# Performer attention and a gated feed-forward block on one Trainium2 core: k chunks taken in opposite order by two engines, loads gated to the projection phase, crossbar transposes moved to the gate phase

## The chip, the cores and the metric

The kernel runs on one core of one Trainium2 chip. The metric is device time in microseconds (us); lower is better. Each time is the median of several executions. The profile of one execution is shown beside it; its span is about 1.8 us shorter than the time of the same execution.

Names: TensorE (PE, with its weight loads PEld) multiplies matrices; VectorE (DVE) and ScalarE (ACT) work elementwise and reduce; POOL is GpSimd, which here issues the loads and builds the identity matrix; SP (SyncE) issues stores and crossbar transposes (a DMA that transposes on its way). PSUM is the memory into which TensorE writes.

Tiles: `pk` and `pq` are the projections of k and q, each taken in five chunks per batch; `k_p` and `q_pT` their exponentials; `v_ext` is v times the weights `wk`; `kz` holds kv and z; `nd` numerator and denominator of the attention, `xt` (`xT`) its transpose; `g_ps` and `v_ps` are the gate and value products, `o_ps` the last projection.

## The reference, cut to what matters

```python
# q, k, v: (8, 8, 576, 64); omega: (128, 64)
def phi(x):
    proj = einsum('bhsd,md->bhsm', x, omega)
    h = proj - sum(x * x, -1) / 2
    return exp(h - max(h, -1)) / sqrt(m)
q_p, k_p = phi(q * scale), phi(k * scale)
kv, z = einsum('bhsm,bhsd->bhmd', k_p, v), sum(k_p, 2)
attn  = einsum('bhsm,bhmd->bhsd', q_p, kv) / (q_p . z + 1e-6)
x   = attn as (4608 tokens, 512)
out = (gelu(x @ w_gate) * (x @ w_val)) @ w_out      # d_ff = 1536
```

## The kernel before

Attention of batch t + 1 is woven into the feed-forward of token tile t (512 tokens). The kernel has a start (attention of batches 0 and 1, gates of tile 0), six steps with attention (t = 1 to 6), two without, and an end (the last projection). Within a step comes first the *projection phase* (48 `o_ps` matmuls of tile t - 1, with k and q chunks between them), then the *gate phase* (12 pairs of `g_ps` and `v_ps`, with `kz` and `nd` between them). The order on PE, ACT and DVE is the program's order.

```python
att = tc.tile_pool(name="att", bufs=2, space=PSUM)   # 2 tiles of 2 banks
mo  = tc.tile_pool(name="mo",  bufs=4, space=PSUM)   # 4 tiles of 1 bank

def k_chunk(self, c):
    i0, n = CHUNKS[c]
    pk = att_tile([P, 2, 4, M], F32, "pk")
    ...                                              # 2n matmuls into pk
    nc.scalar.activation(self.k_p[...], pk[:, :, :n, :], func=Exp)
    nc.vector.reduce_max(self.nmax[...], pk[:, :, :n, :], axis=AX, negate=True)

# end of start(): tile 0's first gates, batch 1's last k chunk done
        n.weights()          # wk = exp(-max), on ACT
        g.gelu(0)
        n.v_half(0)          # v_ext = v * wk, on DVE
        g.mul(0)
        g.gelu(1)
        g.val(1)
        n.v_half(1)
        g.mul(1)
        n.kz()               # needs v_ext
        for jf in range(2, N_DFF): ...

def step(t, before):
    p = Projection(t - 1, before.gated)
    ...
    load_batch(t + 2)                                # k, q, v by POOL
    a = Attention(t + 1)
    a.kT, a.qT = transposed_dma("k", t + 1), transposed_dma("q", t + 1)   # by SP
    a.k_chunk(0); a.k_chunk(1); p.go(15)
    a.k_chunk(2); a.k_chunk(3); p.go(13)
    ...
```

A chunk's `pk` is free for the next chunk but one when both its exponential and its maximum are done.

The softmax here doesn't subtract the row's maximum and nothing guards it: scores larger than these inputs give would overflow.

## Time and profile before

| | before |
|---|---|
| time, median | 368.79 us (3 runs), 368.91 us (4 runs) |
| span of the profile | 366.3 us |
| start, to the first `pk` of step 1 | 63.72 us |
| one step (2 to 6), first `pk` to first `pk` | 37.44 us |
| a step without attention | 31.1 us |
| last matmul to the end of the span | 5.5 us |

Three lines of the page of before: busy time (with the share of the span and the number of instructions), the granted clock of TensorE in 40 equal slices in tenths of full speed (9 is 90% or more), and the engines' shares of the chain of waits that ended last.

```profile
...
PE 344.7 (94%) x2673; PEld 165.6 (45%) x2673; DVE 207.4 (57%) x336; ACT 161.5 (44%) x259; POOL 26.0 (7%) x40
...
PEclk9989699999999999999999999999999999999999
...
PE 78%; DVE 8%; ACT 7%; DMA 5%; issue 1%; POOL 0%; POOLq 0%
...
```

TensorE is busy nearly all the time and carries most of the chain. So a gain has to come from TensorE's waits, or from its clock: one slice, at 37 to 46 us, reads 6.

The timeline of before, TensorE in step 2's projection phase. Columns: start, length, engine, line, operation, output<-inputs, shape, count, and in brackets the idle time ahead and what ended it.

```profile
...
100.99 0.62 PE L196 MATMUL pk<-omegaT_106,kT 64*128 64x128 bf16 x16
101.55 3.41 PE L337 MATMUL o_ps<-w_out_sb,gated 128*128 128x512 bf16 x15
104.89 0.40 PE L196 MATMUL pk<-omegaT_106,kT 64*128 64x128 bf16 x8
105.61 0.40 PE L196 MATMUL pk<-omegaT_106,kT 64*128 64x128 bf16 x8 [0.32 <-DVE nmax L198]
105.94 2.98 PE L337 MATMUL o_ps<-w_out_sb,gated 128*128 128x512 bf16 x13
...
```

The first 16 `pk` matmuls fill both tiles and take 0.56 us (101.55 - 100.99). The next 16 take 1.05 us (105.94 - 104.89): the last eight wait for VectorE's maximum (`nmax`) of an earlier chunk. The waits of the whole kernel (total us, times, longest) say why the maximum comes late:

```profile
...
DVE nmax L198 <- ACT k_p L197: 15.9, 22, 1.8
...
```

It waits for the exponential of the same chunk. Both engines only read, but they read the same PSUM banks. The Trainium skill, "PSUM — Partial Sum Buffer", section "PSUM bank collisions raise a hardware error", says that two engines must not read one bank at once, so the program puts one behind the other; this trace agrees with the 15.9 us above.

The chain of waits of before in the start (start, length, what):

```profile
...
40.41 1.17 PE kz_ps L236 x36
41.58 1.82 PE g_ps L291 x4
43.40 1.62 PE v_ps L304 x4
...
48.48 15.19 DMA kT<-k_in
...
63.72 0.28 PE pk L196 x4
```

`kz` of batch 1 runs at half speed (1.17 us for 36), and so do the next eight gate matmuls (1.82 and 1.62 us for four each; warm it is 0.86). Then, at the end of the start, stands a crossbar transpose that took 15.19 us from issue to landing; TensorE had other work for nearly all of that time and waited only 0.47 us for it. The windows view of before shows the clock (the number ahead of the last two):

```profile
...
core 0: us, PE busy (x) PEld busy (x) DVE busy (x) ACT busy (x) POOL busy (x), PEclk, DMA share, GB/s
36.00:38.00 2.00, 0.09 (x6) 0.10 (x8) 1.55 (x3) 1.89 (x3) 0.64 (x1) 1.00 1.24 207
...
40.00:42.00 2.00, 1.59 (x38) 1.22 (x38) 1.27 (x4) 0.00 (x0) 0.00 (x0) 0.50 1.26 216
...
44.00:46.00 2.00, 2.00 (x16) 0.96 (x15) 0.84 (x3) 0.03 (x1) 0.00 (x0) 0.80 1.23 209
...
```

TensorE idled before (0.09 us busy in 36 to 38), and the clock fell to 0.50 for some 6.8 us. The chain at the end of before:

```profile
...
350.44 10.37 PE o_ps L337 x48
...
360.83 0.69 DVE o_sb L341
```

### The profile page before, as it was taken

How to read it: one execution, taken by the hardware profiler on the slowest of the kernel's cores; microseconds unless marked ns; L12 is line 12 of the kernel's file. 1: busy time of each engine (PE TensorE's matmuls, PEld its weight loads, DVE VectorE, ACT ScalarE, POOL GpSimd, SP SyncE). 2: the span in 40 equal slices, each digit the busy share in tenths (PEclk: the TensorE clock that was granted, in tenths of full speed). 3: DMA queues.
4: the chain of work that ended last, by engine and by line, in shares of the span. 5: the costliest groups of instructions: out<-in, count | busy, mean ns of one | idle time of the engine just before them, and what ended most of it. 6: DMA issues, size and time to landing. Idle time of an engine off the chain costs nothing.

```text
span 366.3 us, 6525 instructions
## 1 busy us (share of the span) xinstructions
PE 344.7 (94%) x2673; PEld 165.6 (45%) x2673; DVE 207.4 (57%) x336; ACT 161.5 (44%) x259; POOL 26.0 (7%) x40
## 2 busy tenths in 40 slices
PE   3787799999999999999999999999999999999993
PEld 2463454445444544354435443544354444444441
DVE  2977584758475847574666567655856333424431
ACT  4877224662367336643664365536453113303310
POOL 8223000201001000100000000000000000000000
PEclk9989699999999999999999999999999999999999
DMA  7999999999618981799079206420312040031013
GB/s 119 271 272 207 207 271 185 249 283 235 87 30 215 209 117 29 185 221 135 23 159 216 44 6 154 104 50 0 87 38 58 7 109 1 1 74 42 0 30 87
DMA packets 64238, 44.11 MB, mean 120 GB/s; under 512 B 44752, under 2 KB 57552, under 8 KB 64208
## 3 DMA queue, kind: packets, MB, share of 16 engines
q0 software_dynamic: 15392, 23.60, 32.0%
q1 hardware_dynamic: 48816, 20.10, 27.6%
q8 instruction: 21, 0.34, 0.4%
q14 instruction: 9, 0.07, 0.1%
HBM read 37.78 MB, written 9.44 MB: 129 GB/s over the span
## 4 chain that ended last, share of the span: by engine, by line
PE 78%; DVE 8%; ACT 7%; DMA 5%; issue 1%; POOL 0%; POOLq 0%
PE g_ps L291 24%; PE v_ps L304 23%; PE o_ps L337 21%; DVE nmax L198 6%; DMA kT<-k_in 4%; PE kz_ps L236 3%; ACT k_p L197 3%; PE nd L251 2%; PE pq L210 2%; PE pk L196 2%; ACT L197 2%; DVE x_sb L259 1%; DMA k_in<-in_k_dram 1%; ACT g_gelu L297 1%; ACT q_pT L213 1%
## 5 line engine op out<-in xcount | busy, mean ns | idle before, releaser
L309 DVE TENSOR_TENSOR gated<-g_gelu,v_ps 128x512 bf16<-128x512 bf16 x108 | 73.7, 687 | 102.1 <-PE v_ps L304 77.3
L297 ACT ACTIVATE g_gelu<-g_ps 128x512 bf16<-128x512 f32 x108 | 63.7, 597 | 142.0 <-PE g_ps L291 141.9
L291 PE MATMUL g_ps<-xT,w_gate_sb 128*128 128x512 bf16 x432 | 111.9, 382 | 0.0
L304 PE MATMUL v_ps<-xT,w_val_sb 128*128 128x512 bf16 x432 | 111.7, 381 | 0.0
L337 PE MATMUL o_ps<-w_out_sb,gated 128*128 128x512 bf16 x432 | 97.9, 380 | 0.0
L304 PEld LDWEIGHTS <-w_val_sb 128*128 128x128 bf16 x432 | 41.8, 98 | 51.9 <-issue 3.0
L337 PEld LDWEIGHTS <-gated 128*128 128x128 bf16 x432 | 40.3, 98 | 50.7 <-issue 4.1
L291 PEld LDWEIGHTS <-w_gate_sb 128*128 128x128 bf16 x432 | 39.6, 98 | 43.1 <-issue 0.6
L198 DVE TENSOR_REDUCE nmax<-pk 128x8 f32<-128x1024 f32 (+1 forms) x40 | 43.3, 1114 | 16.0 <-ACT k_p L197 15.9
L213 ACT ACTIVATE q_pT<-pq 128x512 bf16<-128x512 f32 (+1 forms) x80 | 38.2, 564 | 16.6 <-PE pq L210 16.6
L197 ACT ACTIVATE k_p<-pk 128x1024 bf16<-128x1024 f32 (+1 forms) x40 | 36.1, 937 | 21.0 <-PE pk L196 20.7
L341 DVE COPY o_sb<-o_ps 128x512 f32<-128x512 f32 x36 | 24.7, 686 | 23.5 <-PE o_ps L337 23.0
L259 DVE TENSOR_TENSOR x_sb<-nd,iden 128x512 bf16<-128x512 f32 (+3 forms) x45 | 28.4, 631 | 1.5
L224 DVE TENSOR_TENSOR v_ext<-vf,wk 128x1152 bf16<-128x1152 f32 x16 | 21.7, 1358 | 2.8 <-ACT wk L202 2.8
L196 PE MATMUL pk<-omegaT_106,kT 64*128 64x128 bf16 x288 | 14.9, 228 | 3.8 <-DVE nmax L198 3.0
L251 PEld LDWEIGHTS <-q_pT 128*128 128x128 bf16 (+1 forms) x320 | 13.8, 100 | 10.2 <-DVE x_sb L259 2.5
L251 PE MATMUL nd<-kz,q_pT 128*128 128x65 bf16 (+1 forms) x320 | 15.9, 194 | 0.6 <-ACT kT L163 0.6
L236 PE MATMUL kz_ps<-v_ext,k_p 64*128 64x65 bf16 x576 | 12.5, 203 | 3.9 <-DVE v_ext L226 3.9
L196 PEld LDWEIGHTS <-kT 64*128 64x128 bf16 x288 | 9.3, 97 | 14.6 <-issue 12.6
L236 PEld LDWEIGHTS <-k_p 64*128 64x128 bf16 x576 | 11.4, 103 | 7.1 <-issue 4.0
L210 PE MATMUL pq<-qT,omegaT_106 64*128 64x512 bf16 (+1 forms) x80 | 12.7, 363 | 1.8 <-ACT q_pT L213 1.4
L93 POOL DMA_DIRECT2D vf<-in_v_dram x8 | 6.1, 765 | 78.8 <-DVE v_ext L226 77.0
(34 smaller groups left out, 95.8 us busy)
## 6 DMA issues: line engine op xcount, KB each, us to landing
vf<-in_v_dram POOLq DMA_DIRECT2D x8, 1152.0 KB, 7.7
out_dram<-o_sb SPq DMA_DIRECT2D x72, 128.0 KB, 2.4
q_in<-in_q_dram POOLq DMA_DIRECT2D x8, 576.0 KB, 10.0
k_in<-in_k_dram POOLq DMA_DIRECT2D x7, 576.0 KB, 11.1
w_gate_sb<-in_moe_w_gate_dram POOLq DMA_DIRECT2D x3, 512.0 KB, 20.9
w_val_sb<-in_moe_w_val_dram POOLq DMA_DIRECT2D x3, 512.0 KB, 20.7
w_out_sb<-in_moe_w_out_dram POOLq DMA_DIRECT2D x3, 512.0 KB, 20.3
k_in<-in_k_dram POOLq DMA_DIRECT2D x2, 288.0 KB, 4.7
```

The costliest lines, as they stand in the source:

```text
L196: nc.tensor.matmul(pk[:, a, i, :], self.kT[sl, i0 + i, :], omegaT2[sl])
L197: nc.scalar.activation(self.k_p[:, :, i0:i0 + n, :], pk[:, :, :n, :], func=Exp)
L198: nc.vector.reduce_max(self.nmax[:, :, i0:i0 + n], pk[:, :, :n, :], axis=AX, negate=True)
L213: nc.scalar.activation(dst[:, a, i0:i0 + n], pq[:, a, :n, :].rearrange("m i (e p) -> m i e p", e=2), func=Exp)
L236: nc.tensor.matmul(kz_ps[e][:, j * DP1:(j + 1) * DP1], self.k_p[sl, u % 2, u // 2, :], self.ve[sl, u, :], start=(r == 0), stop=(r == R - 1))
L251: nc.tensor.matmul(nd[h // 4][:n, (h % 4) * DP1:(h % 4 + 1) * DP1], self.q_pT[:, e, u:u + nr, :].rearrange("m r p -> m (r p)"), self.kz_sb ...
L259: nc.vector.tensor_mul(x_sb[:n].rearrange("p (g h d) -> p g h d", g=2, h=4)[:, gs], ndv[:, :, :, :D], iden[:n, gs].broadcast_to((n, gs.sto ...
L291: nc.tensor.matmul(g_ps, w_gate_sb[:, jm, fs], self.xT[:, jm, :], start=(jm == 0), stop=(jm == N_DM - 1))
L297: nc.scalar.activation(g_gelu, self.ps[jf], func=Gelu)
L304: nc.tensor.matmul(v_ps, w_val_sb[:, jm, fs], self.xT[:, jm, :], start=(jm == 0), stop=(jm == N_DM - 1))
L309: nc.vector.tensor_mul(self.gated[:, jf, :], self.gelus[jf], self.vps[jf])
L337: nc.tensor.matmul(self.o_ps, self.gated[:, jf, qq * P:(qq + 1) * P], w_out_sb[:, jf, :], start=(jf == 0), stop=(jf == N_DFF - 1))
```

## The change

Its intent: (1) the two engines take a pair of chunks in opposite order, so that neither waits for the other at the beginning; (2) the loads of batch t + 2 wait for the first exponential of step t, and the crossbar transposes come in the gate phase before they are needed; (3) in the start: the first k load ahead of the identity, `kz` of batch 0 in two halves, two qT copies moved from VectorE or later, `kz` of batch 1 behind two more gate pairs, batch 2 loaded ahead of the output weights; (4) at the end, the last 128 tokens in two half-width pieces whose stores go out on two queues.

```diff
+        def k_pair(self, c):
+            p0, p1 = self.k_proj(c), self.k_proj(c + 1)
+            begun = self.k_exp(*p0)
+            self.k_max(*p1)
+            self.k_exp(*p1)
+            self.k_max(*p0)
+            return begun
 ... loads of the start
-    ident = singles.tile([P, P], BF16); make_identity(nc, ident)
     load_kq("k", 0, parts=2)
+    ident = singles.tile([P, P], BF16); make_identity(nc, ident)
     load_kq("q", 0)
 ...
     load_gv(2)
+    load_kq("k", 2)
+    load_kq("q", 2)
     ...                                  # w_out
+    load_v(2)
 ... start()
         a.q_chunk(2)
+        a.kz(0)
         ...
         qp(1, dve)
+        a.kz(1)
         a.q_chunk(4)
-        a.kz()
-        qp(2, act)
-        qp(3, dve)
         n.q_chunk(0)
         a.nd(0)
         n.q_chunk(1)
+        qp(2, act)
         a.nd(1)
         a.xt(0)
+        qp(3, act)
 ...
-        n.v_half(0)
         g.mul(0)
+        n.v_half(0)
         ...
-        n.kz()
         for jf in range(2, N_DFF):
             g.both(jf)
-            if jf < 7: n.nd(jf - 2)
-            if 2 < jf < 8: n.xt(jf - 3)
+            if jf == 3: n.kz()
+            if 4 <= jf < 9: n.nd(jf - 4)
+            if 5 <= jf < 10: n.xt(jf - 5)
+            if jf == 5: kqT["k", 2] = transposed_dma("k", 2)
+            if jf == 9: kqT["q", 2] = transposed_dma("q", 2)
 ... step()
-        load_batch(t + 2)
-        a.kT, a.qT = transposed_dma("k", t + 1), transposed_dma("q", t + 1)
-        a.k_chunk(0)
-        a.k_chunk(1)
+        a.kT, a.qT = kqT.pop(("k", t + 1)), kqT.pop(("q", t + 1))
+        begun = a.k_pair(0)
+        load_batch(t + 2, begun)         # each load depends on begun
         p.go(15)
-        a.k_chunk(2)
-        a.k_chunk(3)
+        a.k_pair(2)
 ... after a.kz(): kqT["k", t + 2] = transposed_dma("k", t + 2); q's after jf == 5
-    with tc.manual_schedule(engines={E.Activation, E.PE, E.DVE}):
+    with tc.manual_schedule(engines={E.Activation, E.PE, E.DVE, E.SP}):
 ...
-        Projection(N_TOK - 1, g.gated).go(NSUB * N_DFF)
+        Projection(N_TOK - 1, g.gated).end()   # last piece 2 x 256 columns, stores on SP and ACT
```

More of the change, by code (lines that the diff above doesn't have):

```diff
@@ L70, in mo_tile @@
         return mo.tile(shape, dtype, name=name, tag="mo")
-    ident = singles.tile([P, P], BF16)
-    make_identity(nc, ident)
     def rows_of(src, b):
@@ L85, in load_kq @@
         n = HP // parts
-        for c in range(parts):
-            nc.gpsimd.dma_start(out=tv[:, c * n:(c + 1) * n],
-                                in_=rows_of(src, b)[:, c * n:(c + 1) * n])
         loaded[nm, b] = t
+        return [nc.gpsimd.dma_start(out=tv[:, c * n:(c + 1) * n],
+                                    in_=rows_of(src, b)[:, c * n:(c + 1) * n])
+                for c in range(parts)]
     def load_v(b):
         t = ld.tile([P, HP, R * D], F32, name="vf")
-        nc.gpsimd.dma_start(out=t, in_=rows_of(v, b))
         loaded["v", b] = t
+        return [nc.gpsimd.dma_start(out=t, in_=rows_of(v, b))]
     w_gate_sb = singles.tile([P, N_DM, d_ff], BF16)
@@ L110 @@
     load_kq("k", 0, parts=2)
+    ident = singles.tile([P, P], BF16)
+    make_identity(nc, ident)
     load_kq("q", 0)
@@ L187, in two_banks, with k_proj @@
             return [t[:, 0], t[:, 1]], [(slice(0, 2), t)]
-        def k_chunk(self, c):
+        def k_proj(self, c):
             i0, n = CHUNKS[c]
@@ L196, in k_chunk, with k_exp, k_max @@
                     nc.tensor.matmul(pk[:, a, i, :], self.kT[sl, i0 + i, :], omegaT2[sl])
-            nc.scalar.activation(self.k_p[:, :, i0:i0 + n, :], pk[:, :, :n, :], func=Exp)
+            return c, pk
+        def k_exp(self, c, pk):
+            i0, n = CHUNKS[c]
+            return nc.scalar.activation(self.k_p[:, :, i0:i0 + n, :], pk[:, :, :n, :],
+                                        func=Exp)
+        def k_max(self, c, pk):
+            i0, n = CHUNKS[c]
             nc.vector.reduce_max(self.nmax[:, :, i0:i0 + n], pk[:, :, :n, :], axis=AX,
                                  negate=True)
+        def k_chunk(self, c):
+            p = self.k_proj(c)
+            self.k_exp(*p)
+            self.k_max(*p)
+        def k_pair(self, c):
[5 more added lines that the diff above has]
+            return begun
         def weights(self):
@@ L226, in v_half, with kz @@
             nc.vector.tensor_copy(vev[:, isl, :, D], wkv[:, isl])
-        def kz(self):
-            kz_ps, groups = self.two_banks("kz_ps")
-            for j in range(HP):
+        def kz(self, half=None):
+            if half != 1:
+                self.kz_ps = self.two_banks("kz_ps")
+            kz_ps, groups = self.kz_ps
+            for j in range(HP) if half is None else range(2 * half, 2 * half + 2):
                 for r in range(R):
@@ L238, in kz @@
                                          start=(r == 0), stop=(r == R - 1))
-            for gs, t in groups:
+            for gs, t in groups if half != 0 else ():
                 nc.vector.tensor_copy(self.kz_sb[:, gs], t[:, :, :HP * DP1])
@@ L315, in both, with store @@
             self.mul(jf)
-    def store(c0, o_sb):
+    def store(c0, o_sb, ns=slice(0, d_model), queues=(nc.sync, nc.sync)):
         g = c0 // SP
@@ L321, in store @@
             b, r = divmod(g + i, R)
-            nc.sync.dma_start(
-                out=out[b * S:(b + 1) * S, :].rearrange("(p r) m -> r p m", r=R)[r],
+            queues[i].dma_start(
+                out=out[b * S:(b + 1) * S, ns].rearrange("(p r) m -> r p m", r=R)[r],
                 in_=o_sb[i * SP:(i + 1) * SP, :])
@@ L330, in __init__, with end @@
             self.t, self.gated, self.done = t, gated, 0
+        def end(self):
+            self.go((NSUB - 1) * N_DFF)
+            n = d_model // 2
+            for half in range(2):
+                ns = slice(half * n, (half + 1) * n)
+                o_ps = mo_tile([P, n], F32, "o_ps")
+                for jf in range(N_DFF):
+                    nc.tensor.matmul(o_ps, self.gated[:, jf, (NSUB - 1) * P:NSUB * P],
+                                     w_out_sb[:, jf, ns], start=(jf == 0),
+                                     stop=(jf == N_DFF - 1))
+                o_sb = work.tile([P, n], F32, name="o_sb", bufs=3)
+                nc.vector.tensor_copy(o_sb, o_ps)
+                store(self.t * T_TOK + (NSUB - 1) * P, o_sb, ns, (nc.sync, nc.scalar))
         def go(self, n):
@@ L343, in go, with load_batch @@
                 self.done += 1
-    def load_batch(b):
-        load_kq("k", b)
-        load_kq("q", b)
-        load_v(b)
+    kqT = {}
+    def load_batch(b, begun):
+        for dma in load_kq("k", b) + load_kq("q", b) + load_v(b):
+            tc.add_manual_dep(dma.ins, begun.ins.name, mybir.DependencyInfo(
+                mybir.DependencyClass.Sync, mybir.DependencyReason.DATA))
     def start():
@@ L406, in start @@
         n.k_chunk(1)
-        load_batch(2)
         g = Gated(0)
@@ L416, in start @@
         g.gelu(0)
+        g.mul(0)
         n.v_half(0)
-        g.mul(0)
         g.gelu(1)
         g.val(1)
+        g.mul(1)
         n.v_half(1)
-        g.mul(1)
-        n.kz()
         for jf in range(2, N_DFF):
             g.both(jf)
-            if jf < 7:
-                n.nd(jf - 2)
-            if 2 < jf < 8:
-                n.xt(jf - 3)
+            if jf == 3:
+                n.kz()
+            if 4 <= jf < 9:
+                n.nd(jf - 4)
+            if 5 <= jf < 10:
+                n.xt(jf - 5)
+            if jf == 5:
+                kqT["k", 2] = transposed_dma("k", 2)
+            if jf == 9:
+                kqT["q", 2] = transposed_dma("q", 2)
         return g
@@ L441, in step @@
             return g
+        a = Attention(t + 1)
+        a.kT, a.qT = kqT.pop(("k", t + 1)), kqT.pop(("q", t + 1))
+        begun = a.k_pair(0)
         if t + 2 < B:
-            load_batch(t + 2)
-        a = Attention(t + 1)
-        a.kT, a.qT = transposed_dma("k", t + 1), transposed_dma("q", t + 1)
-        a.k_chunk(0)
-        a.k_chunk(1)
+            load_batch(t + 2, begun)
         p.go(15)
-        a.k_chunk(2)
-        a.k_chunk(3)
+        a.k_pair(2)
         p.go(13)
@@ L469, in step @@
         a.kz()
+        if t + 2 < B:
+            kqT["k", t + 2] = transposed_dma("k", t + 2)
         for jf in range(2, N_DFF):
@@ L475, in step @@
                 a.nd(jf - 1)
+            if jf == 5 and t + 2 < B:
+                kqT["q", t + 2] = transposed_dma("q", t + 2)
         return g
     E = mybir.EngineType
-    with tc.manual_schedule(engines={E.Activation, E.PE, E.DVE}):
+    with tc.manual_schedule(engines={E.Activation, E.PE, E.DVE, E.SP}):
         g = start()
```

## The prediction

> **What bounds the kernel now.** TensorE: the page gives it 344.7 of 366.3 us busy and 78% of the chain of waits. The chain has four stretches: a start up to 63.1 us, six steps of 37.45 us (first `pk` matmul at 100.99, 138.44, ...), two steps of 31.1 us without attention, and an end from 350.3 us. Only TensorE's remaining waits can be won:
>
> 1. Steps 2 to 6: the timeline shows the third and fourth k chunks taking 1.05 us of TensorE (104.89 to 105.94) with a 0.32 us wait on the VectorE maximum; unblocked, in step 1, these 16 matmuls take 0.56.
> 2. Step 1 waits 0.47 us for the crossbar-transposed `kT` (15.2 us from issue, among 1.2 MB loads).
> 3. Start: `kz` of batch 1 waits 2.55 and 1.36 us for `v_ext`; after this idling the windows view shows the granted clock at 0.5 from about 38 to 44.8, so the next eight gate/value matmuls take 1.82 + 1.62 us instead of 1.73.
> 4. End: after the last matmul (360.8) come a 0.69 us copy and two stores issued in turn (0.56 each).
>
> **The change, costed.**
> - *Pairs.* The maximum of a chunk waits for its exponential: both read one PSUM tile (the Trainium skill, "PSUM — Partial Sum Buffer", section "PSUM bank collisions raise a hardware error", forbids two engines reading one bank at once; the waits view agrees: `nmax` waits 15.9 us for `k_p`). In opposite order, VectorE's first maximum runs during the table load; both buffers are free about 3.4 us after the first `pk`, instead of 4.4; TensorE needs them at 3.9. Gain 0.49 x 5, about 0.3 in step 1: 2.8 us.
> - *Loads and transposes moved.* No engine time. The DMAs are off the chain except in step 1: gain 0.47. POOL's long waits cost nothing now.
> - *Start.* First k load ahead of the identity: 0.5 us. `kz` in halves fills TensorE's idle time at 16 us, and two qT copies leave the VectorE chain: after what ScalarE's extra copy gives back I count 0.95 in all, load included, at batch 1's first exponential. `kz` of batch 1 goes behind two more gate/value pairs, which hide `v_ext`. Gate 2 still waits for the first gelu (about 3 us idle), so I expect half clock once more, but for one 3.4 us window instead of two (the Trainium skill, "TensorE: Matmul & The Clock Gate", section "Part 1: The HAM clock gate", gives that window; the trace's 17.7 to 20.9 and 38.0 to 44.8 agree). Another 1.95 us; start 2.9 shorter in all.
> - *End.* Half-width last copy and two queues: 0.85 us.
>
> Sum: 2.8 + 0.47 + 2.9 + 0.85 = 7.0 us. Predicted 361.8 us, 80% range 359.0 to 365.0. Chances: faster by over 2% 0.43, within 2% 0.56, slower 0.01.
>
> **What would show each step.** Step period 36.95 (spacing of first `pk`); no `pk` wait on `nmax`; `kT` never waited for; gate 4 of token tile 0 at about 44.4 us (before 47.3), first projection at about 60.9 (before 64.3); half clock once after 35 us; last matmul to end of span about 4.6 us (before 5.5).
>
> **What would make it wrong.** The granted clock at the start: not falling gives 1.5 us more, falling for two windows loses 1.5. Loads in the projection phase, or a q transpose ahead on SyncE's queue, may delay the stores, whose buffers then block VectorE's copies. A late k transpose would stop a step's start.

## The result and the profile after

The changed kernel takes 362.86 us (median of 4 runs, 362.32 to 362.99) against 368.91 us (4 runs). The ratio is 0.9834, 95% interval 0.9817 to 0.9851: 1.7% faster. A ratio here compares the runs of two kernels of the same rounds, so it is not quite the ratio of the medians quoted.

| | before | after | gain | predicted gain |
|---|---|---|---|---|
| start, to the first `pk` of step 1 | 63.72 | 62.03 | 1.69 | 3.37 |
| step 1 to the last two steps' beginning | 224.39 | 221.59 | 2.80 | 2.8 |
| from there to the end | 78.19 | 77.38 | 0.81 | 0.85 |
| span of the profile | 366.3 | 361.0 | 5.3 | 7.0 |

Steps and end gained what was predicted. The start gained 1.7 us less in these two profiles. (The profiled run of before was a quick one: its time was 368.1 us and its span 366.3, whereas the seven executions of it beside e1 to e4 had spans of 366.6 to 367.6. By the medians the miss is about 1 us.)

The page of the changed kernel:

```profile
...
PE 339.9 (94%) x2644; PEld 165.6 (46%) x2685; DVE 207.1 (57%) x336; ACT 162.6 (45%) x260; POOL 26.1 (7%) x40
...
PEclk9999899999999999999999999999999999999999
...
PE 90%; ACT 4%; DMA 2%; DVE 2%; issue 1%; POOL 0%; ACTq 0%; POOLq 0%
...
```

The chain is now 90% TensorE, and no slice of the clock is below 8. Its timeline in step 2's projection phase, same columns:

```profile
...
98.98 0.62 PE L197 MATMUL pk<-omegaT_112,kT 64*128 64x128 bf16 x16
...
102.88 0.62 PE L197 MATMUL pk<-omegaT_112,kT 64*128 64x128 bf16 x16
103.66 2.75 PE L379 MATMUL o_ps<-w_out_sb,gated 128*128 128x512 bf16 x12 [0.16 <-issue]
...
```

Both groups of 16 come in one piece; the wait for `nmax` is gone, and the step is 36.95 us (135.93 - 98.98). VectorE's two maxima of the first pair, in the timeline of VectorE in the changed kernel:

```profile
...
99.76 1.22 DVE L207 TENSOR_REDUCE nmax<-pk 128x8 f32<-128x1024 f32 x1
101.19 1.23 DVE L207 TENSOR_REDUCE nmax<-pk 128x8 f32<-128x1024 f32 x1 [0.21 <-ACT k_p L202]
...
```

The first now runs while ScalarE still loads its table for the exponential (98.84 to 100.12). Both tiles are free at 102.42, 3.44 us after the first `pk`, and TensorE comes for them at 102.88. Before, the second maximum ended 4.57 us after the first `pk` (at 105.56), too late. Over the whole kernel the maximum still waits for exponentials elsewhere, less:

```profile
...
DVE nmax L207 <- ACT k_p L202: 10.3, 17, 1.8
...
```

The chain in the start of the changed kernel:

```profile
...
38.94 1.79 PE g_ps L318 x4
40.73 1.71 PE v_ps L331 x4
...
44.17 1.33 PE kz_ps L263 x59
...
62.10 0.55 PE pk L197 x16
...
```

TensorE ran gate 2 as soon as the first gelu was there, at half speed (1.79 and 1.71 us), and `kz` came later at full speed. `kT` does not stand in this chain. But it had come in only about a microsecond before the first `pk`: the SP queue issued it at 41.16 us, and 19.8 us is the longest time to landing that the profile gives for a kT, so it landed at about 61.0.

```profile
...
41.16 11.78 SPq L150 DMA_TRANSPOSE kT<-k_in  x1
...
```

The clock after 36 us (columns as before; first 36 to 38, then 40 to 42, then 44 to 46):

```profile
...
36.00:38.00 2.00, 0.03 (x1) 0.00 (x0) 0.72 (x2) 1.24 (x2) 0.00 (x0) 1.00 1.23 207
...
40.00:42.00 2.00, 2.00 (x6) 0.73 (x5) 2.00 (x4) 0.60 (x1) 0.00 (x0) 0.50 1.21 207
...
44.00:46.00 2.00, 1.69 (x75) 1.52 (x76) 1.14 (x2) 0.01 (x1) 0.00 (x0) 1.00 1.23 202
...
```

It falls once, for about 3.4 us. At the end, the last copy is half as wide:

```profile
...
353.71 2.63 PE o_ps L367 x24
...
356.37 0.43 DVE o_sb L371
```

What the prediction counted on first in the start did not come. The second half of the first k load (9 transposes that wait for it, the same in both kernels) and batch 1's first exponential, before and after:

```profile
...
8.05 1.14 PE L162 MATMUL kT_ps<-ident,k_in 128*128 128x128 bf16 x9 [0.48 <-DMA k_in<-in_k_dram]
...
28.99 1.02 ACT L197 ACTIVATE k_p<-pk 128x1024 bf16<-128x1024 f32 x1
...
```

```profile
...
8.91 1.14 PE L164 MATMUL kT_ps<-ident,k_in 128*128 128x128 bf16 x9 [1.33 <-DMA k_in<-in_k_dram]
...
29.67 1.02 ACT L202 ACTIVATE k_p<-pk 128x1024 bf16<-128x1024 f32 x1
...
```

The load was issued at 2.06 instead of 2.42 us and still came in 0.86 us later. Batch 1's first exponential ran at 29.67 us (before: 28.99, predicted 0.95 us earlier than that). Two marks of the prediction that follow are late too: gate 4 of tile 0 at about 45.5 us (predicted 44.4) and the first projection at 62.59 (60.9).

### The profile page after: what moved, and what is told of

Read it like the earlier page. It is cut to its first block, busy times and chain, and to the rows that moved or that the text cites. A ratio compares the mean times of both kernels' runs of the same rounds, so it can differ in the third digit from the quotient of the medians.

```text
span 361.0 us, 6509 instructions
## 1 busy us (share of the span) xinstructions
PE 339.9 (94%) x2644; PEld 165.6 (46%) x2685; DVE 207.1 (57%) x336; ACT 162.6 (45%) x260; POOL 26.1 (7%) x40
## 4 chain that ended last, share of the span: by engine, by line
PE 90%; ACT 4%; DMA 2%; DVE 2%; issue 1%; POOL 0%; ACTq 0%; POOLq 0%
PE v_ps L331 26%; PE o_ps L379 26%; PE g_ps L318 25%; PE kz_ps L263 3%; PE nd L278 3%; PE pk L197 3%; PE pq L235 2%; DMA k_in<-in_k_dram 2%; DVE nmax L207 2%; ACT q_pT L238 1%; ACT k_p L202 1%; PE o_ps L367 1%; ACT kT L165 1%; PE xt_ps L302 0%; PE kT_ps L164 0%
## 5 line engine op out<-in xcount | busy, mean ns | idle before, releaser
L318 PE MATMUL g_ps<-xT,w_gate_sb 128*128 128x512 bf16 x409 | 109.6, 382 | 4.0 <-ACT g_gelu L324 2.9
L331 PE MATMUL v_ps<-xT,w_val_sb 128*128 128x512 bf16 x422 | 109.8, 381 | 1.3 <-issue 1.0
L379 PE MATMUL o_ps<-w_out_sb,gated 128*128 128x512 bf16 x412 | 93.8, 379 | 1.1 <-issue 1.0
L379 PEld LDWEIGHTS <-gated 128*128 128x128 bf16 x420 | 39.1, 98 | 49.3 <-issue 4.1
L383 DVE COPY o_sb<-o_ps 128x512 f32<-128x512 f32 x35 | 24.1, 688 | 21.4 <-PE o_ps L379 20.7
L84 POOL DMA_DIRECT2D k_in<-in_k_dram x9 | 6.8, 755 | 172.7 <-ACT k_p L202 169.5
L197 PE MATMUL pk<-omegaT_112,kT 64*128 64x128 bf16 x288 | 13.8, 228 | 1.3 <-DVE nmax L207 0.9
L235 PE MATMUL pq<-qT,omegaT_112 64*128 64x512 bf16 (+1 forms) x80 | 13.7, 391 | 0.8 <-ACT q_pT L238 0.6
L263 PEld LDWEIGHTS <-k_p 64*128 64x128 bf16 x576 | 10.6, 98 | 3.6 <-issue 3.6
L263 PE MATMUL kz_ps<-v_ext,k_p 64*128 64x65 bf16 x576 | 11.7, 197 | 0.1
```

Source lines behind the costliest of these rows:

```text
L197: nc.tensor.matmul(pk[:, a, i, :], self.kT[sl, i0 + i, :], omegaT2[sl])
L263: nc.tensor.matmul(kz_ps[e][:, j * DP1:(j + 1) * DP1], self.k_p[sl, u % 2, u // 2, :], self.ve[sl, u, :], start=(r == 0), stop=(r == R - 1))
L318: nc.tensor.matmul(g_ps, w_gate_sb[:, jm, fs], self.xT[:, jm, :], start=(jm == 0), stop=(jm == N_DM - 1))
L331: nc.tensor.matmul(v_ps, w_val_sb[:, jm, fs], self.xT[:, jm, :], start=(jm == 0), stop=(jm == N_DM - 1))
L379: nc.tensor.matmul(self.o_ps, self.gated[:, jf, qq * P:(qq + 1) * P], w_out_sb[:, jf, :], start=(jf == 0), stop=(jf == N_DFF - 1))
```

## The experiments

All of them gave correct results. Their profiles are compared by the same marks: the landing of the second half of k (when the 9 transposes begin), batch 1's first exponential, and the first `pk` of step 1. Ratios are to the kernel before, in the same rounds.

| run | 2nd half of k | first exp of batch 1 | first `pk` | wait for kT | median us | ratio |
|---|---|---|---|---|---|---|
| before | 8.05 | 28.99 | 63.72 | 0.47 | 368.9 | 1 |
| changed | 8.91 | 29.67 | 62.03 | 0 | 362.86 | 0.9834 |
| e1_ident_first | 8.90 | 29.66 | 62.18 | 0 | 362.48 | 0.9826 |
| e2_same_order | 8.30 | 28.57 | 60.69 | 1.37 | 364.05 | 0.9873 |
| e3_before_pairs | 8.97 | 30.27 | 64.53 | 0 | 366.07 | 0.9924 |
| e4_moves_undone | 7.68 or earlier | 27.57 | 63.24 | 4.92 | 366.07 | 0.9924 |
| e5_after_again | 8.62 | 29.57 | 61.93 | 0 | 362.27 | 0.9834 |
| e6_k2_early | 8.73 | 28.86 | 59.54 | 0 | 361.60 | 0.9834 |
| e7_fill | 8.16 | 27.36 | 59.79 | 2.21 | 360.65 | 0.9790 |
| e8_fill_k2 | 8.10 | 27.51 | 57.49 | 0 | 360.36 | 0.9774 |
| e9_kz1_undone | 8.37 | 28.77 | 62.45 | 0 | 363.02 | 0.9841 |
| e10_fill_k2_spread | 7.45 or earlier | 28.85 | 56.87 | 0 | 358.25 | 0.9705 |
| e11_fill_k2_warm | 8.53 | 29.38 | 57.40 | 0 | 358.41 | 0.9714 |
| e12_kz0_undone | 8.83 | 29.19 | 61.84 | 1.91 | 362.26 | 0.9816 |

### The order of the first loads

```diff
+    ident = singles.tile([P, P], BF16); make_identity(nc, ident)
     load_kq("k", 0, parts=2)
-    ident = singles.tile([P, P], BF16); make_identity(nc, ident)
```

> The changed kernel with the identity built ahead of the first loads again, as before. What is disputed: in the changed kernel's start, the second half of the first k load came in at 8.86 us (8.05 before) although it was issued earlier (2.06, before 2.42), and batch 1's first exponential ran at 29.67 (28.99 before), 1.6 us later than predicted. Theory A (the issue order did it: q's load follows k's 0.2 us sooner and they share the queue): the second half lands at about 8.05, the kernel is 0.4 to 0.9 us faster than the changed one, ratio to before about 0.9815. Rival B (landing times vary from run to run whatever the order): landing anywhere from 7.9 to 8.9, ratio 0.983 to 0.985.

Measured: landing at 8.90 us, the same as changed; 362.48 us, ratio 0.9826 (0.981 to 0.9842). Theory A falls by the landing; the ratio lies between the two and does not decide. Over all runs, the second half landed at 8.05, 8.90 and 8.97 us with the identity first, and anywhere from 7.45 or earlier to 8.91 with k first. The order neither helped nor hurt beyond that scatter. The first half could not go out earlier either: GpSimd issued it at 1.25 us, against 1.28 with the identity ahead of it.

### The pairs

> The changed kernel with each k pair taken in the same order by both engines (exp 0, max 0, exp 1, max 1). Theory A (the opposite order is what frees the PSUM tiles in time): the step grows from 36.95 back to 37.45 us, TensorE waits for the maximum again before the fourth chunk, 2.5 to 3 us slower in all, ratio to before about 0.991. Rival B (the steps gained because loads and transposes moved away): the step stays near 36.95 and the ratio near 0.983.

```diff
             begun = self.k_exp(*p0)
-            self.k_max(*p1)
+            self.k_max(*p0)
             self.k_exp(*p1)
-            self.k_max(*p0)
+            self.k_max(*p1)
```

The timeline of that run: the first `pk` of step 1, and the second pair of step 2.

```profile
...
60.69 0.62 PE L197 MATMUL pk<-omegaT,kT 64*128 64x128 bf16 x16 [1.37 <-DMA kT<-k_in]
...
101.86 0.40 PE L197 MATMUL pk<-omegaT,kT 64*128 64x128 bf16 x8
102.58 0.40 PE L197 MATMUL pk<-omegaT,kT 64*128 64x128 bf16 x8 [0.32 <-DVE nmax L207]
...
```

The wait of 0.32 us is back and the step is 37.44 us (135.41 - 97.97). So the opposite order, and not the moved transfers, shortens the step. The time grew by only about 1.4 us, not the 2.5 to 3 expected: the start of that build was 1.34 us shorter in the profile (60.69 against 62.03), in a part that the edit does not touch; its clock is compared below.

> The kernel before with the opposite order of the pairs alone. Theory A: the step falls to 36.95 us, 2.5 to 3 us faster, ratio to before about 0.9925. Rival B (needs the moved DMAs as well): step 37.3 to 37.45, ratio 0.998 to 1.

The edit is the same pair put into the kernel before (`a.k_pair(0)` and `a.k_pair(2)` in place of four `a.k_chunk`). Measured: 366.07 us, ratio 0.9924 (0.9909 to 0.9939), with both groups of 16 in one piece; the second of step 2:

```profile
...
105.38 0.62 PE L209 MATMUL pk<-omegaT,kT 64*128 64x128 bf16 x16
...
```

The step is 36.95 us. From the first `pk` of step 1 to the last two steps it took 221.59 us (286.12 - 64.53), against 224.39 before. The pairs alone give the 2.8 us predicted, without the moved loads. (The start of this build is the program of before; its first `pk` came 0.8 us later and its first exponential of batch 1 came 1.3 us later, which shows how far the start scatters by itself.)

### Loads and transposes put back

The edit takes `load_batch` and `transposed_dma` back to where they were before, drops the dependency on `begun`, and leaves SP out of the manual schedule; pairs, start and end stay changed.

> The changed kernel with loads and crossbar transposes issued where they were before (no gating on the first exponential, batch 2 loaded after the first k chunks of batch 1), everything else as changed. Theory A (the moves only took away the wait for kT in step 1): step stays 36.95, step 1 begins with a wait for kT of 0.5 to 2.5 us, since the start is now shorter than the 63.7 us at which kT landed before; 0.5 to 2.5 us slower than the changed kernel, ratio 0.985 to 0.990. Rival B (the moves pay in each step): step longer than 37.1. Rival C (worth nothing): ratio 0.983.

```profile
...
63.24 1.04 PE L194 MATMUL pk<-omegaT,kT 64*128 64x128 bf16 x16 [4.92 <-DMA kT<-k_in]
...
```

Measured: 366.07 us, ratio 0.9924 (0.9904 to 0.9944): 3.3 us slower than the changed kernel, more than expected. `kT` is issued at 48.46 us as before and lands 14.7 us later. TensorE, earlier now, waits 4.92 us for it, and after this wait runs at half speed: the 16 `pk` take 1.04 us instead of 0.62, and step 1 takes 39.69 us (102.93 - 63.24) instead of 36.95. Steps 2 to 6 stay at 36.95 us, so the moves pay nothing there. Rivals B and C fall. In the kernel before there was only 0.47 us of this wait to take away, but without the moves the rest of the start's gain is lost to the wait for `kT`: this build beats before by 2.7 us, less than the pairs and the end together (3.6). Loads and transposes were put back together, so this run does not tell which of the two matters.

### The same kernel again

> The changed kernel once more, unchanged. In five profiles so far the second half of the first k load came in anywhere from under 7.7 to 8.97 us, with either issue order, and batch 2's kT at 60.7 to 62.1 us, about 20 us after its issue at 41. Theory A (the start's length differs from run to run by what the loads happen to do, at least 1 us): ratio to before between 0.981 and 0.986, and a start whose first pk differs from 62.03 by up to 1.5 us. Rival B (the start is the same each time): first pk at 62.0 within 0.2 and the ratio at 0.983 to 0.984.

Measured: ratio 0.9834 (0.9813 to 0.9855) and first `pk` at 61.93: by the profile rival B. But its four runs spread from 361.25 to 363.18 us. What follows the first `pk` took 298.8 to 299.0 us in all seven profiles with the changed steps and end and no other loss there (changed, e1, e5, e6, e7, e9, e12), so it is most likely the start that differs from run to run, by more than B allows. What differs can be seen in the profiles of the same instructions in other builds. `kz` of batch 0, two halves, in the changed kernel:

```profile
...
17.15 1.18 PE L263 MATMUL kz_ps<-v_ext,k_p 64*128 64x65 bf16 x36
...
19.76 1.17 PE L263 MATMUL kz_ps<-v_ext,k_p 64*128 64x65 bf16 x36
...
```

and in e7_fill, where that part of the program is the same:

```profile
...
16.46 0.75 PE L263 MATMUL kz_ps<-v_ext,k_p 64*128 64x65 bf16 x36 [0.17 <-DVE v_ext L251]
...
17.97 0.75 PE L263 MATMUL kz_ps<-v_ext,k_p 64*128 64x65 bf16 x36
...
```

36 matmuls take 1.17 us in one and 0.75 in the other (with the last one's tail). These are TensorE's two speeds. The Trainium skill, "TensorE: Matmul & The Clock Gate", section "Part 1: The HAM clock gate", gives 1.2 and 2.4 GHz, says that the faster comes after about 3.4 us of sustained work, and that the window runs freely, so that the turning point varies from run to run. These traces agree on two speeds (four value matmuls of the changed kernel took 1.71 us at 41 us and 0.86 later) and on the length of a slow stretch (about 3.4 us here, 6.8 before); where the window stands, they do not show. In the profiles of the changed start, from the third k chunk's exponential to batch 1's first one, two slow halves go with 18.6 to 18.9 us (changed, e1, e5, e10), one slow and one faster with 18.1 to 18.4 (e2, e6, e9), two fast with 17.1 (e4, e7, e8). That is up to 1.8 us of the start, and it fits the shorter start of e2. The clock record is no help at this place: it says 1.00 from 14 to 22 us in the changed kernel, although its `kz` ran slow there.

The same holds after the idle time at 36 us. Seven profiles have the wait of 2.90 us (within 0.01) for the first gelu. In three of them (changed, e1, e5) the clock then halved for one window; in four (e2, e4, e6, e12) it did not, and the gates ran at 0.86 us for four at once. But with the changed load order that bought nothing: from the first exponential to the first `pk` e2 took 32.12 and e12 32.65 us, waits for `kT` included, against 32.36 in the changed kernel. Only e6, where `kT` comes early, shows the gain (30.68).

### Is the end of the start set by kT?

```diff
     load_v(1)
+    load_kq("k", 2)
     load_gv(1)
     load_gv(2)
-    load_kq("k", 2)
-    load_kq("q", 2)
     for c in range(3): ...     # w_out
+    load_kq("q", 2)
     load_v(2)
```

> The changed kernel with batch 2's k loaded ahead of the second and third thirds of the gate and value weights, and its q behind the output weights. Theory A (the start ends with TensorE waiting for, or just meeting, the transposed kT): kT lands before 57 us, TensorE never waits for it, first pk at 60.0 to 62.0 according to the loads, ratio 0.980 to 0.983. Rival B (TensorE's own work always ends the start): no wait before either, ratio unchanged at 0.983 to 0.985. If the weights now come late, TensorE waits for them at gates 4 or 8 and it is slower.

The SP queue of that run:

```profile
...
31.17 9.25 SPq L150 DMA_TRANSPOSE kT<-k_in  x1
...
```

`kT` is issued 10 us earlier, as soon as k is there, and there is no wait for it. The profiled run was the fastest (360.10 us, first `pk` at 59.54, no half clock at 36 us); the five runs spread to 363.09, and the ratio is unchanged at 0.9834 (0.9813 to 0.9854). So the edit alone has no measurable gain. It takes away a bound. By issue and longest time to landing, `kT` of batch 2 lands at 57.8 to 62.2 us in the builds with the changed load order, in the changed kernel, e1 and e5 1.07, 0.03 and 0.12 us ahead of the first `pk`: TensorE's own work and `kT` end there nearly together. That the bound is there, e2, e12 and the next runs show.

> The changed kernel with gate and value 2 and 3 of token tile 0 put into the PSUM tiles that the k chunks leave free, so that TensorE has work during the 2.9 us in which it waited for the first gelu; kz of batch 1 goes three pairs later. Theory A (after that idling the granted clock halves, and kT of batch 2 is the next bound): no half clock after 35 us, the gate phase of tile 0 ends at about 57 to 58 us, but TensorE then waits for kT until 61 to 62, so at most 1 us is gained, ratio 0.981 to 0.985. Rival B (kT lands earlier when TensorE runs ahead): ratio near 0.972.

```diff
+        for jf in (2, 3):
+            t = att_tile([P, 2, T_TOK], F32, "gv_ps")   # the tiles that the k chunks leave
+            g.gate(jf, t[:, 0]); g.val(jf, t[:, 1])
+            g.gelu(jf); g.mul(jf)
-        for jf in range(2, N_DFF):
+        for jf in range(4, N_DFF):
             g.both(jf)
-            if jf == 3: n.kz()
+            if jf == 6: n.kz()
 ...                                                     # nd and xt in pairs 7 to 11
```

```profile
...
57.28 0.29 PE L302 MATMUL xt_ps<-ident,x_sb 64*128 64x64 bf16 x4
59.79 0.62 PE L197 MATMUL pk<-omegaT,kT 64*128 64x128 bf16 x16 [2.21 <-DMA kT<-k_in]
...
```

The gate phase of tile 0 ends at 57.6 us, TensorE never runs at half speed after 30 us, and then it waits 2.21 us for `kT`, as theory A said. It landed at 59.7 us, a little earlier than I had put it, so the gain is 1.6 us over the changed kernel run beside it (360.65 against 362.27), above the 1 us expected. In the same way e2 waited 1.37 us and e12 1.91 us with an unchanged load order.

> Both of the two edits before together. Theory A: kT has landed when the gate phase of tile 0 ends, first pk at 57 to 58.5 us, 3.5 to 4.5 us faster than the changed kernel, ratio to before 0.972 to 0.975. If q of batch 2 or the output weights come late instead, TensorE waits in step 1 and half of that is lost, ratio about 0.978.

Both edits together: 360.36 us, ratio 0.9774 (0.9754 to 0.9795). No wait for `kT` is left, first `pk` at 57.49. But it is only 0.3 us better than e7, and short of the 0.972 to 0.975 expected (the profiled run, at 358.89 us, was the fastest; the other three took 360.16 to 360.58). In the profile TensorE waits 1.23, 0.59 and 0.61 us for VectorE at 51 to 58.5 us, where I had clustered `nd` and the x transposes; the next run tests this.

> Fill and early k of batch 2 as in the run before, with kz one pair earlier and nd and x transposes spread one per pair, because the clustered ones there made TensorE wait for VectorE 1.23, 0.59 and 0.61 us. Theory A: these three waits go, at most 0.7 us of wait for v_ext comes at kz, first pk at 55.5 to 58, ratio 0.970 to 0.976, about 1.5 us faster than with the clustered ones. Rival B (kT, landing when it likes, sets the end): a wait for kT at the first pk and the ratio stays at 0.977.

```diff
-            if jf == 6: n.kz()
+            if jf == 5: n.kz()
-            # nd and xt in clusters at jf 7 to 11
+            if 6 <= jf < 11: n.nd(jf - 6)
+            if 7 <= jf < 12: n.xt(jf - 7)
```

```profile
...
57.93 0.40 PE L197 MATMUL pk<-omegaT,kT 64*128 64x128 bf16 x8 [0.60 <-DVE xT L305]
...
```

358.25 us, ratio 0.9705 (0.9679 to 0.9732). Two of the three waits are gone; one stays, 0.60 us at the second chunk's `pk`. From the first exponential to the first `pk` it takes 28.02 us, against 29.98 with the clusters. This kernel beats both: 2.9% faster than before, and by the two ratios (0.9705 / 0.9834) about 1.3% faster than the changed kernel, which was not run in the same rounds.

> The same with 18 matmuls of 256 columns on a constant tile in the first 5 us, in which TensorE waits for k. In the profiles so far the kernels fall into two kinds: kz of batch 0 at about 1.1 us per 36 matmuls (half speed) and batch 1's first exponential at 28.9 to 30.3 us, or at about 0.65 and the exponential at 27.4 to 27.6. Theory A (whether the array's clock has come up by 15 us decides this, and it is luck): always the fast kind, exponential at 26.5 to 27.6, spread of the times under 0.5 us, 0 to 1 us faster than without, ratio 0.968 to 0.974. Rival B (the kind comes from the loads): spread and times as without.

```diff
+    warm_sb = singles.tile([P, 256], BF16); nc.vector.memset(warm_sb, 1.0)
+    warm_ps = att_tile([P, 256], F32, "warm_ps")
+    for _ in range(18):
+        nc.tensor.matmul(warm_ps, warm_sb[:, :P], warm_sb, start=True, stop=True)
```

358.41 us, ratio 0.9714 (0.9694 to 0.9735): no better. The clock came up (the first nine transposes took 0.68 us instead of 1.14) and fell again. TensorE had little to do just before (1.07 and 1.28 us of work in 8 to 10 and 10 to 12 us); that this is why it fell was not tested. The windows view of that run, 12 to 16 and 18 to 20 us (the clock is the number ahead of the last two):

```profile
...
12.00:16.00 4.00, 3.12 (x25) 1.62 (x23) 4.00 (x6) 3.54 (x8) 1.11 (x2) 0.68 1.17 246
...
18.00:20.00 2.00, 1.60 (x29) 1.41 (x31) 0.85 (x2) 0.66 (x2) 0.74 (x1) 0.50 1.23 206
...
```

The five runs agree within 0.45 us, as theory A said, but the exponential was late in the profiled one (29.38 us, expected 26.5 to 27.6). The clock is not the only reason: TensorE waited 1.08 us for batch 1's q, until 18.39 us, which no other profile shows.

### Single moves of the start undone

> The changed kernel with kz of batch 1 ahead of gate 2 again and the second v_ext products ahead of the gated products, as before. Theory A (putting kz behind two more gate and value pairs hides the wait for v_ext; the prediction counted 1.95 us): from batch 1's first exponential to the end of tile 0's gates takes about 34 us instead of 32.3, with waits for v_ext of about 2.5 and 1.4 us, 1.5 to 2 us slower, ratio to before 0.988. Rival B (the end of the start is set by kT's landing): first pk stays near 62 and the ratio at 0.983 to 0.985.

```diff
-        g.mul(0); n.v_half(0); g.gelu(1); g.val(1); g.mul(1); n.v_half(1)
+        n.v_half(0); g.mul(0); g.gelu(1); g.val(1); n.v_half(1); g.mul(1)
+        n.kz()
 ...                            # nd from pair 2, xt from pair 3 on, as before
```

```profile
...
37.69 0.75 PE L263 MATMUL kz_ps<-v_ext,k_p 64*128 64x65 bf16 x36 [2.55 <-DVE v_ext L251]
40.19 1.17 PE L263 MATMUL kz_ps<-v_ext,k_p 64*128 64x65 bf16 x36 [1.75 <-DVE v_ext L251]
...
```

The waits for `v_ext` are back. From the first exponential to the first `pk` it takes 33.68 us, 1.32 more than the changed kernel's 32.36 (29.67 to 62.03; in e5 also 32.36). The time is only 0.3 us longer by the ratios (0.9841, 0.9819 to 0.9864), which does not tell it from the changed kernel. The profile shows an exponential 0.9 us earlier than in the changed kernel, in a part that the edit does not touch. How much this move is worth in time is left open.

> The changed kernel with kz of batch 0 whole again and the third and fourth pieces of batch 1's qT where and on the engines they were before. Theory A (these moves gain little, the prediction counted 0.45 us): within 0.7 us of the changed kernel, ratio 0.983 to 0.986, and from the exponential of the third k chunk to batch 1's first one about 18.7 to 19.2 us. Rival B (they gain what the first k load lost, about 1 us or more): ratio 0.987 or more.

The edit makes `kz` of batch 0 whole again after `q_chunk(4)` and puts `qp(2, act)`, `qp(3, dve)` back behind it. Measured: 362.26 us, ratio 0.9816 (0.9794 to 0.9838), not slower than the changed kernel. From the third chunk's exponential to batch 1's first one it takes 18.31 us (29.19 - 10.88), where changed, e1 and e5 take 18.72 to 18.90. That is below what theory A expected (18.7 to 19.2): half of its `kz` ran at the faster speed (72 matmuls in 1.62 us). Theory A holds in its weak form: these moves gained nothing that can be measured here.

## Why the prediction was right, and where it was off

- **Total.** Predicted 361.8 us (359.0 to 365.0) and most likely within 2%; measured 362.86. The range held, the gain was 6.0 instead of 7.0 us.
- **Pairs: right, in mechanism and size.** Predicted 2.8 us and a step of 36.95 us; measured 2.80 us and 36.95. e3 gives the same alone, and e2 loses it.
- **End: right.** Predicted 0.85 us and 4.6 us from the last matmul to the end; measured 0.81 and 4.65 (361.0 - 356.35). The Trainium skill, "DMA: Bandwidth & Descriptors", section "Issuing engines are not separate DMA queues", says that a second issuing engine saves only the time of issuing. Here the narrower copy gave 0.26 us (0.69 - 0.43), and the 0.55 us that remain are what the issue of one store took before (0.56 us, median). No run undid the end alone, but e3, which has the old end, takes the 78.2 us of before from the last two steps' beginning on.
- **"I count 0.95 in all, load included, at batch 1's first exponential": this step failed.** It measured minus 0.68 us in the two profiles (plus 0.60 against e3, whose start is that of before) and about nothing in time: undoing the load order (e1) or the `kz` and qT moves (e12) costs nothing. The load's part, 0.5 us, failed because the identity had held up the issue of the two halves by only 0.03 and 0.36 us, and because the landing of the second scatters by 1.5 us. The rest, 0.45 us, is smaller than the 1.8 us that the clock's state puts into this part; from the third chunk's exponential on, the two profiles take the same (18.68 before, 18.72 changed).
- **`kz` of batch 1, 1.95 us: right by the profiles.** From the first exponential to the end of the gates it went from 34.26 (28.99 to 63.25) to 32.36 us, 1.9 us, with one half-clock window instead of two, as predicted. That it was one was luck in part: four of seven profiles of this start had none. e9, also with one window, puts the term at 1.3 us in its profile, and in time it is not settled.
- **"`kT` never waited for": half right.** The profiled run did not wait, but `kT` came only 1 us ahead, and in two profiles with the same load order and no half clock at 36 us (e2, e12) TensorE waited for it. So the 1.5 us more that the prediction saw in a clock that does not fall were not to be had with this load order. The prediction took 0.47 us, the wait in the kernel before, as the worth of the moves. With the shorter start they are worth 3.3 us (e4), and they moved the bound to about 58 to 62 us rather than away.

What stays open: why the clock's window falls as it does in one build and otherwise in another, and so how the single parts of the start add up to the 2.4 us that it gained by the medians (6.0 - 2.80 - 0.81).

## What to carry to other kernels

Where two engines read the same PSUM tiles, let them take a pair of tiles in opposite order: here it cost nothing that shows and freed the pair about one maximum earlier (3.44 instead of 4.57 us after the first `pk`). When a stretch is shortened, look for what lands just after its present end, here a crossbar transpose 20 us under way among loads, because it may be the next bound; order the loads by when their data is needed and test the two edits together. Idle time of TensorE can cost twice, once by itself and once by the clock after it (here in three of seven profiles). Work put into the gap of 2.9 us (gates in spare PSUM tiles, e10) shortened the way from the first exponential to the first `pk` to 28.0 us, from 32.4 where the clock had halved and 30.7 where it had not (e6).

## What the Trainium skill lacked or had wrong

- "TensorE: Matmul & The Clock Gate" (table "Why this matters for your kernels") advises against idle gaps over about 3 us. A gap of 2.90 us halved the clock in three of seven profiles here and cost about 1.7 us more (e1 and the changed kernel against e6, 32.5 and 32.4 against 30.7 us from first exponential to first `pk`). The page says that the window runs freely; it doesn't say that a gap just under its length can go either way.
- The same page warns not to trust the clock events. These runs show one way in which they mislead: the record reads 1.00 at 14 to 22 us in the changed kernel, while 36 `kz` matmuls take 1.17 us there and 0.75 in other builds.
- The same page advises to warm up with 4 us of matmuls before a benchmark; it gives no share of busy time that keeps the clock up afterwards. In e11 TensorE was busy 2.35 of 4 us at 8 to 12 us (1.07 + 1.28), and the granted clock was 0.68 at 12 to 16 us and 0.50 at 18 to 20, where 36 `kz` matmuls took 1.17 us.
- "DMA: Bandwidth & Descriptors" gives a bandwidth for crossbar transposes, but nothing on how long one takes among loads: a `kT` took 4.1 to 5.9 us from issue to landing (the medians of the runs, mostly steps), and the slowest, that of the start, 14.7 to 20.7.
- No page says how much the landing of a load varies: the same 288 KB load of the start landed anywhere from 7.45 us or earlier to 8.97.
